# Two PSUM copies ahead of a cast, and a store, the turns and a load of rows moved into a y phase, in a two-layer spectral and MLP kernel

## The chip, the cores and the metric

The kernel runs on one core of one Trainium2 chip. The metric is the device time of the program in microseconds, the median of several runs. The core's engines work from queues of their own: TensorE (PE) multiplies, VectorE (DVE) and ScalarE (ACT) work element by element, GpSimd (POOL) takes small pieces, and SyncE (SP) issues every DMA of this kernel, in the order of the program.

## What is computed

```python
def _A_ref(x, dft_seq_re, dft_seq_im, dft_hid_re, dft_hid_im):
    a = jnp.einsum("bsd,ed->bse", x, dft_hid_re)
    b = jnp.einsum("bsd,ed->bse", x, dft_hid_im)
    y = jnp.einsum("ts,bse->bte", dft_seq_re, a) - jnp.einsum("ts,bse->bte", dft_seq_im, b)
    return y
def _B_ref(x, w1, w2, w3, w4):
    ...  # h = gelu(layernorm(x) @ w1), its four quarters shifted by +1, -1, +2, -2 rows
    x1 = x + hs                      # hs = shifted h @ w2
    return x1 + _gelu(_layernorm(x1, axis=-1) @ w3) @ w4
x = x + _A_ref(_layernorm(x, axis=-1), ...)
x = x + _B_ref(_layernorm(x, axis=-1), ...)
x = x + _A_ref(_layernorm(x, axis=-1), ...)
x = x + _B_ref(_layernorm(x, axis=-1), ...)
```

x is 1 x 2048 x 512 in 32-bit floats; the inner width of the MLP is 1376.

## The kernel before

**Precision.** Every operand is split into a high part (a cast to the fast 32-bit matmul type) and a low part (the rest). A product is three matmuls, high x high, high x low, low x high (`mm3`, L295 to L297), so PE's second matmul of a product is the first to read the streamed operand's low part.

**Fourier layers.** The kernel does the sequence transform first. It walks over 4 chunks of 512 output columns (c = 0 to 3), and in each chunk over 8 pairs of row tiles (k). Chunk 0 of layer 0 is a plain phase; every other chunk has an *x phase* (`x_phase`), then a *y phase* (`y_phase`). The two use sums and differences of the blocks of the sequence matrices, so that fewer products are needed. The phases share the eight PSUM banks, in pairs PA, PB, PC, PD (psa to psd in the profile). At the end of the x phase ACT copies PC, PB and PA to SBUF (L518, L520, L526), since the y phase writes the same banks anew. In the x phases of c = 1 to 3 also the hidden transform of the chunk before is computed (`hid`, on PD). The last chunk's hidden transform stands alone behind the last y phase: four pieces of the hidden matrices, 24 matmuls each (`HORDER`), with the left operands im0, re1, im1 and re0 (buffers rr) in this order. Then comes the MLP (`by_pairs`).

**The stream.** The blocks of the matrices come through a ring of 4 buffers. A piece is loaded into one of 4 raw buffers (6 from late in the x phase to the end of the y phase; raw_180 to raw_185 in the lists below) by `issue_dma`, L223, as soon as all users of the piece that had it have run. `stage_one` makes a block's high part. In the y phase it is a DVE subtraction of two raw halves (L247, written to ring...f) and an ACT cast (L248). `stage_two` makes the low part on DVE (L258). `stream()` hands PE the next block; before that it runs `stage_one` of the blocks ahead, up to 4 buffers, and `stage_two` of all but the newest. So on DVE the subtraction of a block stands ahead of the low part of the block before it. The y phase has 16 blocks, two a pair, of 12 matmuls each.

**Work beside the stream.** The program's order on each engine is written by hand: the phases call hooks between the blocks (`hook(i)` in the x phase with i = 2k and 2k + 1, `hook(k)` in the y phase). In layer 0 they also prepare sums of MLP weights that DRAM keeps for later: a *sum unit* is loaded, summed, split and stored (`sum_load`, `sum_make`, `sum_low`, `sum_keep`), at steps given to `sum_at`; step 16 + k lies in the y phase. The buffer suma of such a unit lies at the same SBUF address as turned0.

**In the last chunk** (c = 3) the hooks also start the MLP's input: rows of the finished sum x come back from DRAM (`BACK`: step of the x phase and first row tile), four row tiles are normalized (L354) and *turned* (32 x 32 block transposes on DVE, L632) into turned0, four DMAs store that to zd (`turn_out`, L642), and one load brings it back as the MLP's left operand (`turn_in`, L647, in the y phase's last hook).

Of the kernel before, what the change touches and what calls it, by code (L numbers as in the profile page):

```python
# [21 lines left out]
NC = S // CH  # L22
# [14 lines left out]
WARM = 12  # L37
X6, X7 = 2, 4
HAT = (2, 3, 3, 4, 5, 5, 6, 6)
BACK = {8: 0, 11: 2, 13: 4}  # L40
HORDER = ((1, 0), (0, 1), (1, 1), (0, 0))


# [1 line left out]
def spectral_mlp_kernel(ctx: ExitStack, tc: tile.TileContext, x, ws, hs, w1, w2, w34, out):  # L45
    nc = tc.nc
# [9 lines left out]
    x1d = dram.tile([S, D], F32, name="x1d")  # L56
# [28 lines left out]
    def at(name, word, *shape, dtype=F32R):  # L85
        return nc.alloc_sbuf_tensor_at(name, [P, *shape], dtype, offset=base + 4 * word).ap()
# [4 lines left out]
    tmp = at("tmp", TMP, 6, D, dtype=F32)  # L91
# [6 lines left out]
    xs = [at(f"xs{i}", XS + i * 2 * D, 2, D, dtype=F32) for i in range(NP)]  # L98
    turned0 = at("turned0", 5 * AY, KD, CH, dtype=F32)
# [25 lines left out]
    def xt(j):  # L125
        return xs[j // 2][:, j % 2]
# [22 lines left out]
    pieces, items, w_items, w_pieces, y_pieces = [], [], [], [], set()  # L149
# [43 lines left out]
            uses.setdefault(i, []).append((n, "two" if it[0] == "plain" else "one"))  # L193
    raws, slots, sums = {}, {}, {}
    held = {i: None for i in range(len(raw_at))}
    state = {"wide": False, "dma": 0, "one": 0, "two": 0, "use": 0, "made": 0, "done": 0, "limit": 0, "load": w_pieces[0]}
    x_left = [(0, 1), (1, 1)] + [(j, 2) for j in range(2, NT, 2)]

    def load_x():
        if x_left:  # L200
            j, n = x_left.pop(0)
            rows(xs[j // 2][:, j % 2 : j % 2 + n], x, j, n, True)

    def rows(sb, d, j, n, load):
        v = d[j * P : (j + n) * P, :].rearrange("(t p) d -> p t d", p=P)
        nc.sync.dma_start(*((sb, v) if load else (v, sb)))

    def issue_dma(upto=None):
        while state["dma"] < (state["load"] if upto is None else upto):
            i = state["dma"]  # L210
            free = [
                r
                for r, p in held.items()
                if (r < RAW or state["wide"] and i in y_pieces)
                and (p is None or all(n < state[stage] for n, stage in uses[p]))
            ]
            if not free:
                break
            src, a, b = pieces[i]
            r = min(free, key=lambda r: (-1 if held[r] is None else held[r], r))  # L220
            held[r] = i
            raws[i] = raw_at[r]
            nc.sync.dma_start(raws[i][:, a:b], src)  # L223
            state["dma"] += 1
            if i % 2 and i > 3:
                load_x()

    def stage_one():

        n = state["one"]  # L230
        kind, ids, (a, b), dest = items[n]
        issue_dma()
        if dest is None:
            dest = ring[state["made"] % RING]
            sums[n] = ringf[state["made"] % RING][:, :, 1]
            state["made"] += 1
        slots[n] = dest
        r = [raws[i] for i in ids]
        lo = sums.get(n)
        if kind == "plain":  # L240
            nc.scalar.copy(dest[:, a:b, 0], r[0][:, a:b])  # L241
        elif kind == "one":
            nc.vector.tensor_tensor(lo[:, 0], r[0][:, 1], r[0][:, 0], op=ALU.subtract)
            nc.scalar.copy(dest[:, 0, 0], lo[:, 0])  # L244
        else:
            i = 1 if kind == "by1" else 0
            nc.vector.tensor_tensor(lo, r[1][:, i : i + 1].broadcast_to([P, 2, CH]), r[0], op=ALU.subtract)  # L247
            nc.scalar.copy(dest[:, :, 0], lo)  # L248
        state["one"] += 1
        issue_dma()  # L250

# [18 lines left out]
    def prefetch():  # L270
        n = state["one"]
        while room():
            stage_one()
            while state["two"] < state["one"] - 1:
                stage_two()
        while state["two"] < n:
            stage_two()
# [5 lines left out]
    def stream():  # L283
        i = state["use"]
        if i and items[i - 1][3] is None:
            state["done"] += 1
        state["use"] += 1
        prefetch()
        while state["two"] <= i:
            stage_two()  # L290
        return slots.pop(i)
# [61 lines left out]
    def normed_act(o, s, mr):  # L353
        nc.scalar.activation(o, s, AF.Identity, bias=mr[2], scale=mr[1])  # L354
# [139 lines left out]
    def run_late(*names):  # L494
        for i in names:
            for f in late.pop(i, ()):
                f()

    def x_phase(c, hook):
        h = 0  # L500
        for k in range(NP):
            first, last = k == 0, k == NP - 1
            while c and h < NP and HAT[h] == k:
                s = stream()
                ri, dp = HORDER[h % 4]
                hid(ri, dp, s, PD, 2 * (h // 4), h % 4 == 0, h % 4 == 3)
                if h % 4 == 3:
                    at_mix = c == NC - 1 and h > 4
                    add_y(c - 1, h // 4, PD, X1 if h > 4 else X0, 2 * k + 1 if h < 4 else "y", "10" if at_mix else 2 * k + 2 if h < 4 else "y+")
                h += 1  # L510
            s = stream()
            run_late(2 * k)
            hook(2 * k)
            mm_half(PC, ax[k][:, 2], s[:, 0], first, last)
            mm_half(PB, ax[k][:, 1], s[:, 1], first, last)
            if last:
                for i in range(2):
                    nc.scalar.copy(im1s[:, i], PC[i])  # L518
                for i in range(2):
                    nc.scalar.copy(re1s[:, i], PB[i])  # L520
            s = stream()
            run_late(2 * k + 1)
            hook(2 * k + 1)
            mm_half(PA, ax[k][:, 0], s[:, 0], first, last)
        for i in range(2):
            nc.scalar.copy(re0s[:, i], PA[i])  # L526
# [64 lines left out]
    ln1, ln2 = {}, {}  # L591
# [35 lines left out]
    def blocks_of(u):  # L627
        return u.rearrange("p (d a i) -> p d a i", d=KD, a=NB)

    def turn_one(t, q, u):  # L630
        v = t.rearrange("p d (a q j) -> p d a q j", a=NB, q=TC)[:, :, :, q]
        nc.vector.transpose(v, blocks_of(u))  # L632

    def turn_out(t, to=None):

        if to is None:
            count["turn"] += 1
            to = zd[count["turn"] % 2]
        z = to.rearrange("(e i) t -> i e t", i=B)
        for b in range(NB):  # L640
            v = t[b * B : (b + 1) * B].rearrange("i d (a t) -> i (d a) t", a=NB)
            nc.sync.dma_start(z[:, :, b * P : (b + 1) * P], v)  # L642
# [973 lines left out]
    sum_a = [(*both("suma", 5 * AY, 4, 2, 2 * P), slice(0, 4))]  # L1616
# [45 lines left out]
    def sum_at(c, kind, k, places, *at_):  # L1662
        todo = (
            lambda: sum_load(kind, k, places),
            lambda: sum_make(kind, places),
            lambda: sum_low(places),
            lambda: sum_keep(kind, k, places),
        )
        for step, f in zip(at_, todo):
            prepare.setdefault((c, step), []).append(f)  # L1670
# [4 lines left out]

    for c, units in ((1, ((3, 0), (3, 1), (3, 2))), (2, ((3, 3), (3, 4), (4, 0))), (3, ((4, 1), (4, 2)))):
        sum_at(c, *units[0], sum_b, 5 if c == 1 else 0, 8 if c == 1 else 7, 9 if c == 1 else 8, 9)
        sum_at(c, *units[1], sum_a, 1, 10, 11, 12 if c == 3 else 21)
        if c < 3:
            sum_at(c, *units[2], sum_t, 11, 13, 14, 18)  # L1680
    sum_at("hid", 4, 3, sum_b, 0)
# [2 lines left out]
    for layer in range(LAYERS):  # L1684
# [4 lines left out]
        for c in range(NC):  # L1689
# [90 lines left out]
            def hook(i):  # L1780
# [34 lines left out]
                if i == 9:  # L1815
                    rows(X0, x1d, j, 2, False)
                if c == NC - 1 and i in BACK:
                    rows(xs[BACK[i] // 2], x1d, BACK[i], 2, True)
                if c == NC - 1 and i == 12:
# [5 lines left out]
            def hook(k):  # L1825
                if layer == 0:
                    prepare_at(c, 2 * NP + k)
                if layer and c == 0:
                    for step, f in zip((1, 1, 2), (ay_sums, ay_highs, ay_lows)):
                        if k == step:  # L1830
                            f(7)
                if k == 1 and c:
                    rows(X1, x1d, (c - 1) * TC + 2, 2, False)
                if c == NC - 1 and k < 2:
                    for q in (2 * k, 2 * k + 1):
                        turn_one(turned0, q, tmp[:, q])
                    for j in (2, 3)[: 2 - 2 * k]:
                        normed_act(tmp[:, j], xt(j), ln2[j])
                if c == NC - 1 and k == 2:
                    turn_out(turned0)  # L1840
                if c == NC - 1 and k == NP - 1:
                    turn_in(ztf[0])

# [7 lines left out]
        for i, (ri, dp) in enumerate(HORDER):  # L1851
# [8 lines left out]
            if i < 3:  # L1860
                j = (6, 8, 10)[i]
# [68 lines left out]
```

## Time and profile before

| | us |
|---|---|
| median of 3 runs | 1419.08 (1418.76 to 1419.23) |
| the profiled execution: its own time | 1418.97 |
| the profiled execution: span of its instructions | 1417.2 |

The span runs from the first to the last instruction in the trace; 1.8 us of the execution's time lie outside it. Times of the trace are microseconds from the span's start. A row of the timeline gives start, length, engine, line, operation, output <- inputs, shapes, the number of merged instructions (xN), and in brackets how long the engine was idle before it and what ended that. A length runs from an instruction's start to its end; a matmul of 512 columns shows 0.39, but the next starts 0.23 after it, since they are pipelined. The length in a row of SP is that of the issue alone; when the data have landed is told by the line "DMA to landing".

### The profile page before, as it was taken

To read this page: it belongs to the slowest core of one execution; us is meant where nothing else is said; L and a number is where in the kernel's file an instruction comes from. 1 tells how busy PE (TensorE), PEld (TensorE's weight loads), DVE (VectorE), ACT (ScalarE), POOL (GpSimd) and SP (SyncE) were. 2 spreads that over 40 slices of the span, in tenths; PEclk is the share of its full clock that TensorE was granted. 3 is DMA by queue.
4 is the path that set the end of the run, shared out by engine and by line. 5 is a ranking of instruction groups with operands and counts; after the bars stand their busy time and mean duration, and the time that the engine had idled before them with its cause. 6 is when DMAs were issued, how large, how long until landed. Compare 5 with 4: busy or idle time off the path is not lost.

```text
span 1417.2 us, 18479 instructions
## 1 busy us (share of the span) xinstructions
PE 1409.0 (99%) x6669; PEld 1181.8 (83%) x6669; DVE 1191.3 (84%) x1684; ACT 765.5 (54%) x1072; POOL 68.2 (5%) x105
## 2 busy tenths in 40 slices
PE   9999999999999999999999999999999999999998
PEld 8888788888788888988888888888888888899887
DVE  7988998998988789956789979879889788897776
ACT  6664555556566655534555545645555566454351
POOL 2100000000001100000000000000000020000000
PEclk9999999999999999999999999999999999999999
DMA  8978858778774748865556476565587457687864
GB/s 290 306 236 302 268 194 274 241 230 309 255 228 146 253 165 264 257 247 180 195 177 218 136 225 206 166 220 170 193 265 237 134 141 245 188 250 252 297 205 160
DMA packets 158907, 316.18 MB, mean 223 GB/s; under 512 B 10848, under 2 KB 78816, under 8 KB 156896
## 3 DMA queue, kind: packets, MB, share of 16 engines
q1 hardware_dynamic: 158816, 315.01, 67.9%
q8 instruction: 52, 0.85, 0.2%
q14 instruction: 39, 0.32, 0.1%
HBM read 260.70 MB, written 54.26 MB: 222 GB/s over the span
## 4 chain that ended last, share of the span: by engine, by line
PE 94%; DVE 3%; DMA 1%; ACT 1%; issue 1%; SPq 0%; POOL 0%; DVEq 0%; ACTq 0%; POOLq 0%
PE psd L295 10%; PE psd L296 10%; PE psd L297 10%; PE psa L295 8%; PE psa L297 8%; PE psa L296 8%; PE psb L296 7%; PE psb L297 7%; PE psb L295 7%; PE psc L295 6%; PE psc L296 6%; PE psc L297 6%; DMA raw<-in_ws 1%; DVE ring L258 1%; DVE rest L492 0%
## 5 line engine op out<-in xcount | busy, mean ns | idle before, releaser
L241 ACT CAST ring<-raw 128x1024 fp32r<-128x1024 f32 x127 | 132.9, 1052 | 69.4 <-PE psd L297 30.6
L258 DVE TENSOR_TENSOR ring<-raw,ring 128x1024 fp32r<-128x1024 f32 x126 | 153.4, 1220 | 14.3 <-ACT ring L241 14.3
L295 PE MATMUL psd<-ring,rr 128*128 128x512 f32 x208 | 80.9, 389 | 0.0
L296 PE MATMUL psd<-ring,rr 128*128 128x512 f32 x208 | 80.9, 389 | 0.0
L297 PE MATMUL psd<-ring,rr 128*128 128x512 f32 x208 | 80.9, 389 | 0.0
L248 ACT CAST ring<-ring0f 128x1024 fp32r<-128x1024 f32 x28 | 29.5, 1054 | 46.9 <-DVE ring0f L247 46.9
L258 DVE TENSOR_TENSOR ring<-ring1f,ring 128x512 fp32r<-128x512 f32 (+1 forms) x56 | 53.3, 952 | 0.8 <-ACT ring L244 0.7
L346 POOL TENSOR_TENSOR rows<-ve,mhalf 128x4 f32<-128x4 f32 x16 | 18.2, 1136 | 735.2 <-DVE ve L345 735.2
L295 PE MATMUL psc<-ring,ay 128*128 128x512 f32 x128 | 50.0, 391 | 1.6 <-ACT rr11f L518 1.6
L296 PE MATMUL psb<-ring,ay 128*128 128x512 f32 x128 | 50.0, 391 | 1.2 <-DVE ring L258 1.2
L297 PE MATMUL psb<-ring,ay 128*128 128x512 f32 x128 | 49.8, 389 | 0.0
L295 PE MATMUL psb<-ring,ay 128*128 128x512 f32 x128 | 49.8, 389 | 0.0
L296 PE MATMUL psc<-ring,ay 128*128 128x512 f32 x128 | 49.8, 389 | 0.0
L297 PE MATMUL psc<-ring,ay 128*128 128x512 f32 x128 | 49.8, 389 | 0.0
L297 PE MATMUL psa<-ring,ay 128*128 128x512 f32 x126 | 49.0, 389 | 0.0
L295 PE MATMUL psa<-ring,ay 128*128 128x512 f32 x126 | 49.0, 389 | 0.0
L295 PE MATMUL psd<-ring,ay 128*128 128x512 f32 x126 | 49.0, 389 | 0.0
L296 PE MATMUL psd<-ring,ay 128*128 128x512 f32 x126 | 49.0, 389 | 0.0
L296 PE MATMUL psa<-ring,ay 128*128 128x512 f32 x126 | 49.0, 389 | 0.0
L297 PE MATMUL psd<-ring,ay 128*128 128x512 f32 x126 | 49.0, 389 | 0.0
L314 POOL TENSOR_TENSOR rs<-ve,mhalf 128x2 f32<-128x2 f32 (+2 forms) x33 | 28.5, 863 | 412.4 <-DVE nb L313 393.4
L697 DVE TENSOR_TENSOR rg<-gt,rg 128x512 fp32r<-128x512 f32 x32 | 22.1, 690 | 29.6 <-ACT rg L696 29.6
(834 smaller groups left out, 4617.1 us busy)
## 6 DMA issues: line engine op xcount, KB each, us to landing
raw<-in_ws SPq DMA_DIRECT2D x183, 512.0 KB, 5.4
raw<-in_hs SPq DMA_DIRECT2D x56, 512.0 KB, 3.7
w3b<-w3d SPq DMA_DIRECT2D x11, 1792.0 KB, 8.5
w4r<-w4d SPq DMA_DIRECT2D x22, 512.0 KB, 3.5
un<-w4s SPq DMA_DIRECT2D x40, 256.0 KB, 3.7
un<-w4d SPq DMA_DIRECT2D x38, 256.0 KB, 4.4
x1d<-tmp SPq DMA_DIRECT2D x12, 512.0 KB, 6.8
xs<-x1d SPq DMA_DIRECT2D x12, 512.0 KB, 5.2
```

Of the source, the lines that this page charges most:

```text
L241: nc.scalar.copy(dest[:, a:b, 0], r[0][:, a:b])
L248: nc.scalar.copy(dest[:, :, 0], lo)
L258: nc.vector.tensor_tensor(lo, src, hi.bitcast(F32), op=ALU.subtract)
L295: nc.tensor.matmul(o, lh, rh, start=first, stop=False, skip_group_check=more)
L296: nc.tensor.matmul(o, lh, rl, start=False, stop=False, skip_group_check=more)
L297: nc.tensor.matmul(o, ll, rh, start=False, stop=last, skip_group_check=more)
L314: nc.gpsimd.tensor_tensor(rs[:, :n], ve[:, :n], mhalf[:, 0, :n], op=ALU.pow)
L346: nc.gpsimd.tensor_tensor(rs, ve, mhalf[:, :, :2], op=ALU.pow)
L697: nc.vector.tensor_tensor(lo, src, hi.bitcast(F32), op=ALU.subtract)
```

## The change

The two copies of PC at the end of each x phase go ahead of the cast of the y phase's second block: a block's cast is put in a list, and run at once unless `hold` is set, as it is in the last k of an x phase. The store of the last suma unit, (4, 2), goes from step 12 (x phase of chunk 3) to step 18 (y phase, k = 2). The load of row tiles 4 and 5 into xs[2] leaves the x phase (step 13) and goes into the y phase at k = 3, in both layers. In layer 0 the turns go from k = 0 and 1 to k = 3 and 5, and their store from k = 2 to k = 5; in layer 1 they stay. No work is added or removed.

```diff
-BACK = {8: 0, 11: 2, 13: 4}
+BACK = {8: 0, 11: 2}
...
+    casts = []
+
+    def cast_held():
+        while casts:
+            casts.pop(0)()
...
-            nc.scalar.copy(dest[:, :, 0], lo)
+            casts.append(lambda: nc.scalar.copy(dest[:, :, 0], lo))
+            if not state["hold"]:
+                cast_held()
...
+            state["hold"] = last
             s = stream()
...
             if last:
                 for i in range(2):
                     nc.scalar.copy(im1s[:, i], PC[i])
+                state["hold"] = False
+                cast_held()
                 for i in range(2):
                     nc.scalar.copy(re1s[:, i], PB[i])
...
-        sum_at(c, *units[1], sum_a, 1, 10, 11, 12 if c == 3 else 21)
+        sum_at(c, *units[1], sum_a, 1, 10, 11, 18 if c == 3 else 21)
...
-                if c == NC - 1 and k < 2:
-                    for q in (2 * k, 2 * k + 1):
-                        turn_one(turned0, q, tmp[:, q])
-                    for j in (2, 3)[: 2 - 2 * k]:
-                        normed_act(tmp[:, j], xt(j), ln2[j])
-                if c == NC - 1 and k == 2:
-                    turn_out(turned0)
+                if c == NC - 1:
+                    turns = (0, 1, 2) if layer else (3, 5, 5)
+                    if k in turns[:2]:
+                        for q in (0, 1) if k == turns[0] else (2, 3):
+                            turn_one(turned0, q, tmp[:, q])
+                    if not k:
+                        for j in (2, 3):
+                            normed_act(tmp[:, j], xt(j), ln2[j])
+                    if k == turns[2]:
+                        turn_out(turned0)
+                if c == NC - 1 and k == 3:
+                    rows(xs[2], x1d, 4, 2, True)
```

The lists below show what stands on an engine one behind the other. Line numbers of the changed program are its own (L254 there is L248 before, L266 is L258, L253 is L247, L643 is L632, L653 is L642).

ACT at the end of chunk 3's x phase in layer 0, before: psc is PC, psb is PB, ring...f the differences of the y phase's blocks.

```order
L248 CAST ring_172<-ring0f 128x2x512
L248 CAST ring_174<-ring1f 128x2x512
L518 COPY rr11f<-psc_249 128x512
L518 COPY rr11f<-psc_250 128x512
L520 COPY rr01f<-psb_247 128x512
```

The same place in the changed program:

```order
L254 CAST ring_172<-ring0f 128x2x512
L527 COPY rr11f<-psc_249 128x512
L527 COPY rr11f<-psc_250 128x512
L254 CAST ring_174<-ring1f 128x2x512
L531 COPY rr01f<-psb_247 128x512
```

The cast of block 1 went behind the two copies of psc; the same holds at all seven ends of x phases.

SP at the same place, before: w4s<-suma is the sum unit's store, xs_147<-x1d the load of rows, raw_184 and raw_185 take the pieces of the y blocks 4 and 5.

```order
L223 DMA raw_183<-in_ws 128x1024
L1655 DMA w4s_87<-suma 128x2048
L1598 DMA w3d_83<-tmp 256x1x256
L206 DMA xs_147<-x1d 128x2x512
L223 DMA raw_184<-in_ws 128x1024
L223 DMA raw_185<-in_ws 128x1024
```

And changed:

```order
L223 DMA raw_183<-in_ws 128x1024
L1609 DMA w3d_83<-tmp 256x1x256
L223 DMA raw_184<-in_ws 128x1024
L223 DMA raw_185<-in_ws 128x1024
L223 DMA raw_180<-in_ws 128x1024
```

The store and the load of rows went out from ahead of raw_184; the short store w3d<-tmp stayed.

SP further on in chunk 3's y phase, before: raw_180 and raw_181 here take the pieces of pair 6 (blocks 12 and 14), zd<-turned are the turns' four stores, in_hs is the hidden matrices.

```order
L206 DMA x1d<-tmp 128x2x512
L223 DMA raw_180<-in_ws 128x1024
L223 DMA raw_181<-in_ws 128x1024
L642 DMA zd_73<-turned_153 32x16x128 x4
L223 DMA raw_182<-in_ws 128x1024
L223 DMA raw_183<-in_ws 128x1024
L223 DMA raw_180<-in_hs 128x1024
L223 DMA raw_181<-in_hs 128x1024
```

And changed:

```order
L206 DMA x1d<-tmp 128x2x512
L223 DMA raw_180<-in_ws 128x1024
L223 DMA raw_181<-in_ws 128x1024
L1666 DMA w4s_87<-suma 128x2048
L223 DMA raw_182<-in_ws 128x1024
L223 DMA raw_183<-in_ws 128x1024
L206 DMA xs_147<-x1d 128x2x512
L653 DMA zd_73<-turned_153 32x16x128 x4
L223 DMA raw_180<-in_hs 128x1024
L223 DMA raw_181<-in_hs 128x1024
```

The sum unit's store now stands where the turns' stores stood, and these stand directly ahead of the hidden matrices.

DVE in the same y phase, before: the first turns stand ahead of the subtraction of block 4.

```order
L258 TENSOR_TENSOR ring_176<-ring2f,ring_176 128x2x512
L632 STREAM_TRANSPOSE turned_153<-tmp 128x16x32 x2
L247 TENSOR_TENSOR ring0f<-raw_185,raw_184 128x2x512
L258 TENSOR_TENSOR ring_178<-ring3f,ring_178 128x2x512
L247 TENSOR_TENSOR ring1f<-raw_185,raw_184 128x2x512
```

In the changed program they stand behind the low part of block 8 (ring_172), and ahead of the subtraction of block 10 (ring2f):

```order
L266 TENSOR_TENSOR ring_172<-ring0f,ring_172 128x2x512
L643 STREAM_TRANSPOSE turned_153<-tmp 128x16x32 x2
L253 TENSOR_TENSOR ring2f<-raw_185,raw_184 128x2x512
L266 TENSOR_TENSOR ring_174<-ring1f,ring_174 128x2x512
L253 TENSOR_TENSOR ring3f<-raw_185,raw_184 128x2x512
L266 TENSOR_TENSOR ring_176<-ring2f,ring_176 128x2x512
L500 TENSOR_TENSOR rr00f<-rr00f,rr11f 128x2x512
```

The first of these transposes waits for the store w4s<-suma, before and after. The second pair went from behind the low part of block 4 to behind that of block 12. PE's and POOL's lists are the same in both programs.

## Rows read from the trace of the kernel before

**Rows 1.** The page, part 1: busy time, share of the span, instructions

```profile
PE 1409.0 (99%) x6669; PEld 1181.8 (83%) x6669; DVE 1191.3 (84%) x1684; ACT 765.5 (54%) x1072; POOL 68.2 (5%) x105
```

**Rows 2.** PE's waits, whole span: total us, times, longest

```profile
PE psc L295 <- ACT rr11f L518: 1.6, 2, 0.8
...
PE psb L296 <- DVE ring L258: 1.2, 1, 1.2
```

**Rows 3.** Timeline of PE, chunk 1's and chunk 2's change to y

```profile
148.16 0.39 PE L297 MATMUL psa<-ring,ax 128*128 128x512 f32 x1
149.31 0.50 PE L295 MATMUL psc<-ring,ay 128*128 128x512 f32 x1 [0.76 <-ACT rr11f L518]
...
152.42 0.40 PE L296 MATMUL psb<-ring,ay 128*128 128x512 f32 x1
...
251.55 0.40 PE L296 MATMUL psb<-ring,ay 128*128 128x512 f32 x1
```

**Rows 4.** Timeline of ACT, chunk 1's change to y

```profile
148.68 1.07 ACT L518 COPY rr11f<-psc 128x512 f32<-128x512 f32 x2
```

**Rows 5.** Timeline of DVE, chunk 1's and chunk 2's change to y

```profile
150.96 1.22 DVE L258 TENSOR_TENSOR ring<-ring1f,ring 128x1024 fp32r<-128x1024 f32 x1
...
250.07 1.22 DVE L258 TENSOR_TENSOR ring<-ring1f,ring 128x1024 fp32r<-128x1024 f32 x1
```

**Rows 6.** Timelines of ACT and DVE, layer 1, chunk 1's change to y

```profile
849.52 1.05 ACT L248 CAST ring<-ring1f 128x1024 fp32r<-128x1024 f32 x1 [0.68 <-DVE ring1f L247]
...
851.69 1.22 DVE L258 TENSOR_TENSOR ring<-ring1f,ring 128x1024 fp32r<-128x1024 f32 x1
```

**Rows 7.** Timeline of PE, chunk 3's y phase and the hidden phase's first matmul

```profile
346.57 0.39 PE L295 MATMUL psc<-ring,ay 128*128 128x512 f32 x1
...
354.73 0.39 PE L295 MATMUL psb<-ring,ay 128*128 128x512 f32 x1
356.27 0.50 PE L296 MATMUL psb<-ring,ay 128*128 128x512 f32 x1 [1.15 <-DVE ring L258]
...
391.94 0.39 PE L295 MATMUL psc<-ring,rr 128*128 128x512 f32 x1
```

**Rows 8.** Timeline of DVE, chunk 3's y phase

```profile
349.86 1.22 DVE L258 TENSOR_TENSOR ring<-ring2f,ring 128x1024 fp32r<-128x1024 f32 x1
350.99 1.30 DVE L632 STREAM_TRANSPOSE turned<-tmp 128x512 f32<-128x512 f32 x2
353.86 1.23 DVE L247 TENSOR_TENSOR ring0f<-raw,raw 128x1024 f32<-128x1024 f32 x1 [1.57 <-DMA raw<-in_ws]
```

**Rows 9.** Timeline of SP, end of chunk 3's x phase

```profile
341.45 1.02 SPq L1655 DMA_DIRECT2D w4s<-suma  x1
343.52 0.52 SPq L1598 DMA_DIRECT2D w3d<-tmp  x1
...
345.62 0.95 SPq L223 DMA_DIRECT2D raw<-in_ws  x1
```

**Rows 10.** Chunk 2's loads; landings of L1655's stores issued 262.46, then 341.45

```profile
261.61 0.81 SPq L223 DMA_DIRECT2D raw<-in_ws  x2
...
DMA to landing us min/median/max: 9.2/9.2/9.2
...
DMA to landing us min/median/max: 7.3/7.3/7.3
```

**Rows 11.** SP, the turns' stores; landings of L223's loads issued 367.87, then 380.21

```profile
364.02 3.73 SPq L642 DMA_DIRECT2D zd<-turned  x4
...
DMA to landing us min/median/max: 7.4/7.4/7.4
...
DMA to landing us min/median/max: 3.6/3.6/3.6
```

**Rows 12.** Timelines of ACT and DVE, start of the hidden phase: parts of im0

```profile
387.37 1.05 ACT L450 CAST rr<-rr10f 128x1024 fp32r<-128x1024 f32 x1
...
388.46 1.23 DVE L453 TENSOR_TENSOR rr<-rr10f,rr 128x1024 fp32r<-128x1024 f32 x1
```

More of the change, by code (lines that the diff above doesn't have):

```diff
@@ L195, in spectral_mlp_kernel @@
     held = {i: None for i in range(len(raw_at))}
-    state = {"wide": False, "dma": 0, "one": 0, "two": 0, "use": 0, "made": 0, "done": 0, "limit": 0, "load": w_pieces[0]}
+    state = {"wide": False, "hold": False, "dma": 0, "one": 0, "two": 0, "use": 0, "made": 0, "done": 0, "limit": 0, "load": w_pieces[0]}
     x_left = [(0, 1), (1, 1)] + [(j, 2) for j in range(2, NT, 2)]
```

## The prediction

> **What bounds the kernel now.** I read the busy times first: TensorE (PE) is busy for 1409.0 of 1417.2 us, and DVE for 84% [rows 1]. So a change of order can win only the time in which PE stands still, about 8 us, part of it at the start and in the MLP. The list of PE's waits says where the rest lies: two waits of the psc banks for ACT's copies (L518) and one of a psb bank for DVE's L258 [rows 2]. They fall at the end of the x phases of chunks 1 and 2 of layer 0, and in the y phase of chunk 3. The timeline of PE gives their size. At chunk 1 the next matmul comes 1.15 us after the one before it, where 0.23 is usual, so 0.92 is lost, and 0.11 more because a matmul after a wait takes 0.50 instead of 0.39 [rows 3]. Chunk 2 is built alike. In chunk 3 the y phase starts at 346.57 and its blocks take 2.72 each (354.73 less 346.57, over three blocks). Without a wait the hidden phase would begin after 16 blocks, at 390.09; it begins at 391.94 [rows 7]. So 1.85 us are lost there, and all three places together hold about 3.95 us: the most that the change can give.
>
> I number the 16 y blocks of a chunk from 0. Block n needs sub(n) (DVE, L247), cast(n) (ACT, L248) and low(n) (DVE, L258). In program order sub(n+1) stands ahead of low(n), and PE's second matmul of block n, 0.23 after its first, needs low(n). A DVE operation starts 1.14 after the one before (349.86 to 350.99) and ends 1.22 after its start [rows 8].
>
> **The copies ahead of the cast.** At chunk 1 ACT copies psc at 148.68, behind a cast [rows 4]. With the copies first PE may start block 0 about 0.9 us earlier. But then DVE ends the gain: its order and its work are untouched, it runs without a gap here, and low(1) runs from 150.96 to 152.18 [rows 5]. PE's second matmul of block 1 is now at 152.42 [rows 3]; it can come down to 152.23 (0.05 from DVE to PE, as from DVE's low(3), which ended at 356.22 by the spacing above, to PE at 356.27), and then pays the 0.11 of a restart. That is a gain of 0.08. At chunk 2 low(1) ends at 251.29 against 251.55 on PE [rows 3, 5]: a gain of 0.10. Together 0.2 of the 2.1 us that lie there; I take 0.2, because DVE's rows are closer than the wait's own length, and keep 2.1 as the other end. The same swap at chunk 3 and four times in layer 1 costs nothing: in layer 1 the cast starts at 849.52, could move by the 1.07 of two copies at most, and would end at 851.64; DVE reads it at 851.69 [rows 4, 6]. PE has no wait there now [rows 2].
>
> **The store and the load out of the x phase.** In chunk 3 SP issues the sum unit's store (1.02), a short store that waits for DVE until 343.52, the load of rows, and only then, at 345.62, the loads for blocks 4 and 5 [rows 9]. Their landing ends DVE's idle 1.57 us ahead of sub(4) at 353.86, behind the first two turns (1.30) [rows 8]. Without them the loads go out from 344.1, the second at 344.5. Now they are there at 353.86, 8.24 after the first's issue; even with that they would land at 352.3, and low(3) would end 1.14 + 1.22 later, at 354.7. PE wants it at 354.96, 0.23 into block 3. Without the store and the rows ahead of them they should be earlier, about when DVE comes free of low(2), at 351.0. So the whole 1.85 us goes. (The short store keeps its place: the loads can't go earlier than 344.1.)
>
> **The store in the y phase.** It lies now behind the two loads for pair 6 (blocks 12 and 14), and these wait for sub(7). From sub(4) at 351.0, six operations of 1.14 later sub(7) starts at 357.85 and ends at 359.1. The first two turns write the memory that the store reads, so DVE waits at them until it has landed; behind them on DVE stand sub(10) and low(9). How long that is, the same place in chunk 2 shows: two loads at 261.61, a store of the same 1 MB behind them, landed 9.2 after its issue at 262.46, so 10.05 after the first load [rows 10]. That gives 369.15 here. The other bound is the store as it is now, 7.3 after its issue [rows 10]: 359.95 + 7.3 = 367.3. I take the first, which has the same two loads ahead. When must the turns start? Block 9 starts at 346.57 + 9 x 2.72 = 371.05, its second matmul at 371.28; turns 1.21, sub(10) 1.14, low(9) 1.22 and 0.05 to PE make 3.62. So 367.66. The wait costs 369.2 - 367.66 = 1.55, with the restart 1.66 (0 at the lower bound). DVE then has 2.72 - 2.28 = 0.44 a block to catch up; in blocks 10 to 13 it has also an add (L492, 1.14) and the second pair of turns (1.21) to do, 2.35 against 1.76. That is 0.6 more, as one or two short waits.
>
> The Trainium skill ("DMA: Bandwidth & Descriptors", Anatomy of one DMA — SWDGE (gpsimd) path) prices a DMA at about 2.0 us plus its bytes at 436 GB/s; this is for the other issuing path. An estimate by it is 4.4 us for this 1 MB, a landing at 364.4 and no wait. The trace does not agree: it shows 7.3 and 9.2.
>
> **The turns' own store.** The second pair of turns comes nine DVE operations behind the first: 369.2 + 1.21 + 9 x 1.14 = 380.65, ended at 381.95. Then SP issues the four stores of turned rows (3.73) and only then the first load of the hidden weights, which now lies far behind them [rows 11]. It goes out at 385.7 and lands, at the 3.6 it takes on an idle queue, at 389.3 [rows 11]. ACT's next cast waits for it, and behind that cast stand two copies and the cast of im0 (L450): 1.05 + 1.0 + 1.05, so im0's high part is there at 392.5, its low part (L453, 1.23) at 393.8 [rows 12]. PE reaches the hidden phase at 390.09 + 1.66 + 0.6 = 392.35 and reads the low part 0.45 later, at 392.8: about 0.15 for the one, 0.7 for the other, 0.2 for two restarts, and some 0.4 for the copies and re1 behind. Taken: 1.5. Now im0 has room: high part begun at 387.37, low part at 388.46, for 391.94 [rows 7, 12]. Bounds: 0, if the turns start early; and if the load lands as it did behind these stores in the y phase, 7.4 after its issue [rows 11], 3.8 more. I take the lower landing, since nothing else is queued by then. The load of rows itself, 0.5 MB between loads that have time, costs nothing in either layer; layer 1 keeps its turns.
>
> **Sum.** Gone: 1.85 + 0.2. New: 1.66 + 0.6 + 1.5 = 3.76. Net +1.7 on the profiled execution's 1418.97, or 1420.7; the median of the runs is 0.11 above that execution. Forecast 1420.8.
>
> **Rivals.**
> - The store lands in time (turns not held, start by 366). DVE's own pace would have them at 365.2. Then 2.05 us are won and about 0.1 comes back in the hidden phase: 1417.1. For it: the 7.3 us row is near; against it: the chunk 2 row, with the same neighbours. The price that the Trainium skill states above would give this case. 0.13.
> - The turns wait, but the hidden phase has enough room: +2.26 - 2.05 = +0.2, 1419.3. For it: the first of its waits comes out at only 0.15; against it: the low part follows 1.3 behind the high part. 0.14.
> - Slower: the first load of hidden weights is held by the turns' stores and lands late. At half way between 3.6 and 7.4 us it adds 1.9: 1422.7. It decides from a landing at about 390.5 on. For it: the one row of a load behind such stores; against it: that load had two others ahead. 0.20.
> - The copies pay in full (2.1) and the store lands in time: 1415.2. Against it: DVE's unbroken row of work. 0.03.
> - The forecast, 1420.8, own range 1419.8 to 1421.9: 0.50. That the change doesn't do what it says is excluded by the order: only these instructions move, PE's order stays.
>
> **How the numbers follow.** About 0.2% (2.84 us) is what a measurement of this kernel can tell from no change, so the bounds are 1416.2 and 1421.9. Faster 0.03, slower 0.20, the three cases between 0.77. The range leaves out the 0.03 below and about half of the slower case: 1417.0 to 1422.6.
>
> **What would show it.** Right: at the ends of the x phases of chunks 1 and 2 PE waits for DVE L258 instead of ACT; no wait at 356; DVE idle some 4 us ahead of the first turns of layer 0, released by the store; a PE wait at about 371 and one at the start of the hidden phase on ACT or DVE. Wrong: the store landing before 367.6, or the hidden loads issued by 383; and if DVE's low(1) starts earlier than now, the copies are worth more than 0.2.

## The result, and the profile after

| | us | ratio to before, 95% interval |
|---|---|---|
| before, median of the runs beside it | 1418.76 | |
| after, median of 7 runs | 1423.27 (1422.79 to 1425.07) | 1.0032 (1.0022 to 1.0042) |
| after, the profiled execution (span) | 1425.07 (1423.1) | |

The change costs 4.5 us; the forecast was +1.7, its range ended at 1422.6. The profiled execution is the slowest of the seven; why, is told below.

PE's busy time and PE's waits in the profile of the changed kernel (total us, times, longest), beside [rows 1, 2]:

```profile
PE 1412.6 (99%) x6669; PEld 1182.2 (83%) x6669; DVE 1191.6 (84%) x1684; ACT 764.9 (54%) x1072; POOL 68.6 (5%) x105
...
PE psc L303 <- ACT rr L458: 2.6, 1, 2.6
PE psb L304 <- DVE ring L266: 2.5, 3, 1.7
```

The two waits for ACT's copies are gone. In their place stand short waits for DVE, one longer one, and a new one for the cast of im0 (L458). PE is also *busy* 3.6 us longer, with the same 6669 matmuls: some of them ran slower.

Timeline of PE (start, length, then as in the rows of before): the second matmul of block 1 at chunk 2, the first wait in chunk 3's y phase, and the start of the hidden phase.

```profile
250.77 0.50 PE L304 MATMUL psb<-ring,ay 128*128 128x512 f32 x1 [0.38 <-DVE ring L266]
...
372.50 0.50 PE L304 MATMUL psb<-ring,ay 128*128 128x512 f32 x1 [1.74 <-DVE ring L266]
...
394.69 0.80 PE L303 MATMUL psc<-ring,rr 128*128 128x512 f32 x1 [2.55 <-ACT rr L458]
395.28 0.63 PE L304 MATMUL psc<-ring,rr 128*128 128x512 f32 x1
395.95 0.80 PE L305 MATMUL psc<-ring,rr 128*128 128x512 f32 x1
396.54 0.63 PE L303 MATMUL psc<-ring,rr 128*128 128x512 f32 x1
396.97 0.63 PE L304 MATMUL psc<-ring,rr 128*128 128x512 f32 x1
397.40 0.63 PE L305 MATMUL psc<-ring,rr 128*128 128x512 f32 x1
```

No row like the second of these stands at 356 any more, where [rows 7] have the old wait. The hidden phase's matmuls are 0.63 or 0.80 long where the first one in [rows 7] has 0.39. The first three start 0.59 to 0.67 after one another, those from the fourth on 0.43, where 0.23 is usual. The table of stretches says why (busy us of each engine with its instructions, granted clock, DMA share, GB/s):

```profile
388.00:392.00 4.00, 4.00 (x19) 3.09 (x17) 1.82 (x2) 0.32 (x1) 0.00 (x0) 1.00 0.96 334
392.00:394.60 2.60, 0.14 (x1) 0.00 (x0) 1.23 (x1) 2.60 (x5) 0.00 (x0) 0.96 1.02 395
394.60:401.30 6.70, 6.57 (x15) 4.75 (x16) 6.53 (x6) 5.65 (x9) 0.00 (x0) 0.51 0.75 265
401.30:405.00 3.70, 3.70 (x18) 3.06 (x17) 2.58 (x3) 2.23 (x3) 0.00 (x0) 1.00 0.86 238
```

The granted clock falls late in the wait (0.96 over its 2.6 us), is 0.51, the 1.2 GHz level, over the next 6.7 us, and 1.00 again afterwards. The Trainium skill ("TensorE: Matmul & The Clock Gate", Wait — 56ns, not 53.3ns?) gives 426.7 ns from start to start for 512 columns at this level; the trace agrees with its 0.43.

DVE and SP: the first turns, and the turns' stores with the loads of the hidden matrices behind them. Below them, when the sum unit's store (issued at 359.09) and the first hidden load (384.86) have landed, counted from the issue.

```profile
368.90 1.30 DVE L643 STREAM_TRANSPOSE turned<-tmp 128x512 f32<-128x512 f32 x2 [4.13 <-DMA w4s<-suma]
...
381.64 3.12 SPq L653 DMA_DIRECT2D zd<-turned  x4
384.86 3.40 SPq L223 DMA_DIRECT2D raw<-in_hs  x4
...
DMA to landing us min/median/max: 9.8/9.8/9.8
...
DMA to landing us min/median/max: 6.4/6.4/6.4
```

To see where time comes and goes I set the same matmul of the two traces side by side, by its place in PE's order, and take the difference of the start times at the end of each section. This is the ledger, in us against the kernel before. "Start" is what the two executions differ by at 20 us (in the second trace of the changed kernel, by 100 us), ahead of all that was changed; it comes and goes from run to run.

| kernel | start | chunks 1, 2 | old wait, chunk 3 | store's wait | knock-ons | hidden phase |
|---|---|---|---|---|---|---|
| after | -0.52 | -0.16 | -1.84 | +2.03 | +0.53 | +6.09 |
| after, once more | +0.39 | -0.27 | -1.85 | +1.62 | +0.53 | +4.86 |

All the rest of the program changes it by less than 0.2. The first trace is that of the slowest run: by the medians (+4.5, of which the other columns make 0.56) the hidden phase costs about 4 in a usual run.

### The profile page after: what moved, and what is told of

The parts are those of the page before. It is cut to its first block, busy times and chain, and to the rows that moved or that the text cites. A ratio compares the mean times of both kernels' runs of the same rounds, so it can differ in the third digit from the quotient of the medians.

```text
span 1423.1 us, 18484 instructions
## 1 busy us (share of the span) xinstructions
PE 1412.6 (99%) x6669; PEld 1182.2 (83%) x6669; DVE 1191.6 (84%) x1684; ACT 764.9 (54%) x1072; POOL 68.6 (5%) x105
## 4 chain that ended last, share of the span: by engine, by line
PE 90%; DVE 5%; DMA 2%; issue 1%; ACT 1%; SPq 0%; DVEq 0%; POOL 0%; ACTq 0%; POOLq 0%
PE psd L303 9%; PE psd L305 9%; PE psd L304 9%; PE psa L305 8%; PE psa L303 8%; PE psa L304 8%; PE psb L304 6%; PE psb L305 6%; PE psb L303 6%; PE psc L303 6%; PE psc L305 6%; PE psc L304 6%; DVE ring L266 1%; DVE rest L500 1%; DMA w4s<-suma 1%
## 5 line engine op out<-in xcount | busy, mean ns | idle before, releaser
L247 ACT CAST ring<-raw 128x1024 fp32r<-128x1024 f32 x127 | 132.7, 1051 | 74.6 <-PE psd L305 29.1
L266 DVE TENSOR_TENSOR ring<-raw,ring 128x1024 fp32r<-128x1024 f32 x126 | 153.4, 1221 | 16.9 <-ACT ring L247 16.9
L266 DVE TENSOR_TENSOR ring<-ring1f,ring 128x512 fp32r<-128x512 f32 (+1 forms) x56 | 53.4, 953 | 0.8 <-ACT ring L250 0.7
L254 ACT CAST ring<-ring0f 128x1024 fp32r<-128x1024 f32 x28 | 29.5, 1054 | 45.5 <-DVE ring0f L253 45.5
```

The source lines that it names most:

```text
L254: casts.append(lambda: nc.scalar.copy(dest[:, :, 0], lo))
L266: nc.vector.tensor_tensor(lo, src, hi.bitcast(F32), op=ALU.subtract)
```

## The experiments

**The copies alone.** The changed kernel with the rest put back:

```diff
-BACK = {8: 0, 11: 2}
+BACK = {8: 0, 11: 2, 13: 4}
...
-        sum_at(c, *units[1], sum_a, 1, 10, 11, 18 if c == 3 else 21)
+        sum_at(c, *units[1], sum_a, 1, 10, 11, 12 if c == 3 else 21)
...
-                    turns = (0, 1, 2) if layer else (3, 5, 5)
+                    turns = (0, 1, 2)
...
-                if c == NC - 1 and k == 3:
-                    rows(xs[2], x1d, 4, 2, True)
```

> Only the two psc copies ahead of the y block's cast; the store, the turns and the load of rows stand where they stood in the kernel before. Theory (DVE's unbroken row of work ends the gain): in the trace of the changed kernel PE regains 0.04 us at chunk 1 and 0.08 at chunk 2, so here 0.12 us below the kernel before, about 1418.7, not to be told from no change; PE waits at chunk 1 and chunk 2 for DVE's low part (L266), and the wait of 1.8 us in chunk 3 is back. Rival (ACT's copies were what PE waited for, so the whole wait goes): 2.1 us below, about 1416.7.

Measured: 1418.7 against 1419.27, ratio 0.9995 (0.9986 to 1.0004). In the ledger -0.29 at chunks 1 and 2, and +0.16 in chunk 3, where the old wait for the loads is only reached sooner. So the copies give 0.13 by the trace, as expected; the medians can't tell it from no change.

**The same with one DVE operation taken out of the row.** To test that it is DVE which keeps the rest:

```diff
-            sum_at(c, *units[2], sum_t, 11, 13, 14, 18)
+            sum_at(c, *units[2], sum_t, 11, 13, 17, 18)
```

> The kernel with the copies alone, and the third sum unit's low part three steps later at chunks 1 and 2; chunk 3 as in the kernel before. Theory (the two copies give 0.12 alone because DVE's row of work holds PE next): with one DVE operation out of that row the waits at DVE's low part go, 0.64 at each of two chunks: 1.4 below the kernel before, about 1417.9. Rival (the copies' value was never there, PE's next limit is something else): 0.1 below, about 1419.2.

Measured: 1417.65 against 1418.87, 0.9990 (0.9981 to 0.9998). Its list of PE's waits keeps the one in chunk 3 alone:

```profile
PE psb L304 <- DVE ring L266: 1.4, 1, 1.4
PE psd L140 <- POOL ident masks.py:199: 1.4, 1, 1.4
```

The ledger has -1.57 at chunks 1 and 2. The theory holds: the value was there, 1.28 us of it, behind a DVE operation that PE does not need at that point.

**The store back in the x phase, the turns late.**

```diff
-        sum_at(c, *units[1], sum_a, 1, 10, 11, 18 if c == 3 else 21)
+        sum_at(c, *units[1], sum_a, 1, 10, 11, 12 if c == 3 else 21)
```

> The changed kernel with the last sum unit's store back in the x phase of chunk 3; the late turns and the late load of rows stay. Theory (the store's landing holds the turns, and all that follows comes of that): no DVE wait at the first turns, they start by 366, the turned rows are stored by 382, the hidden phase begins on time at full clock; the loads for blocks 4 and 5 go out 1.0 later than in the changed kernel, so of the old 1.85 us wait some 0.8 is back. Sum: 0.12 + 1.05 below the kernel before, about 1417.7. Rival (late turns by themselves make the hidden load late): the store's wait of 2.0 and the knock-ons of 0.5 go, a wait of 1.5 or more at the hidden phase stays, with the half clock behind it: 1420 to 1422.

Measured: 1421.04 against 1419.27, 1.0008 (0.9999 to 1.0016). The eleven runs spread from 1419.16 to 1421.87, and the traced one (1421.74) is among the slowest. My theory, 1417.7, fell: every run lies above it. The rival came out. DVE is not held at the turns, yet the hidden phase loses 4.18 in the ledger. At DVE's own pace the second turns end at 379.24; the stores go out until 382.4, and the first hidden load, issued at 382.49, lands 6.1 later:

```profile
DMA to landing us min/median/max: 6.1/6.1/6.1
```

The first and the third matmul of the hidden phase, and the stretches around its start (columns as above):

```profile
392.12 0.50 PE L303 MATMUL psc<-ring,rr 128*128 128x512 f32 x1 [1.45 <-ACT rr L458]
...
393.38 0.51 PE L305 MATMUL psc<-ring,rr 128*128 128x512 f32 x1 [0.53 <-DVE rr L461]
...
390.30:393.70 3.40, 1.42 (x5) 0.59 (x4) 2.71 (x3) 3.40 (x5) 0.00 (x0) 1.00 1.05 404
393.70:397.10 3.40, 3.40 (x9) 2.61 (x8) 3.30 (x4) 2.35 (x6) 0.00 (x0) 0.51 0.90 325
```

PE stood idle for 1.45 and once more for 0.53, and then had the half clock for 3.4 us. So late turns are enough to spoil the hidden phase; the store's wait only adds to their lateness. The 4.18 is this trace's: by the medians (+1.77, with 1.05 won ahead of it) the loss is about 2.8. Of the old wait 0.81 stays won, which I put down to the moved rows, and the other 1.03 to the store (its issue took 1.02 [rows 9]).

**The idle time filled.** To part the wait from the slow matmuls behind it:

```diff
+        if layer == 0:
+            for _ in range(11):
+                nc.tensor.matmul(PC[0], ay[7][:, 0, 0, :P], ay[7][:, 0].rearrange("p r d -> p (r d)"), start=True, stop=True)
         for i, (ri, dp) in enumerate(HORDER):
```

> The changed kernel with eleven more matmuls of 128x512 on PE, on operands that are there, into a bank that the hidden phase overwrites, between the last y block of layer 0 and the hidden phase: they fill the 2.7 us in which PE stands idle. Theory (the slow matmuls of the hidden phase come from the clock that fell when PE stood still): granted clock 1.0 throughout, the hidden phase's matmuls 0.227 us apart, its first real matmul again at about 394.7; the total is 2.8 us below the changed kernel's profiled run, that is some 3.2 above the kernel before by the trace. Rival (the matmuls are slow because the hidden loads and the turns' transfers crowd the memory that PE reads): 0.427 apart as before, the total stays at the changed kernel's 1423 to 1425.

Measured: 1422.97 against 1419.27, 1.0024 (1.0015 to 1.0033). Stretches with and behind the filling, and the first real matmuls:

```profile
391.20:394.00 2.80, 2.80 (x14) 2.24 (x13) 1.48 (x2) 2.80 (x5) 0.00 (x0) 1.00 1.00 383
394.00:401.00 7.00, 6.47 (x28) 4.44 (x26) 6.90 (x7) 5.56 (x8) 0.00 (x0) 1.00 0.79 272
```

```profile
393.86 0.41 PE L303 MATMUL psc<-ring,rr 128*128 128x512 f32 x1
394.11 0.40 PE L304 MATMUL psc<-ring,rr 128*128 128x512 f32 x1
395.03 0.50 PE L305 MATMUL psc<-ring,rr 128*128 128x512 f32 x1 [0.53 <-DVE rr L461]
395.36 0.39 PE L303 MATMUL psc<-ring,rr 128*128 128x512 f32 x1
395.60 0.40 PE L304 MATMUL psc<-ring,rr 128*128 128x512 f32 x1
```

The DMA share is 0.79 where the changed kernel had 0.75, the operands are the same, and the matmuls that don't wait run 0.23 to 0.25 apart at a clock of 1.00. So the slowness is the clock, not crowded memory, and it came of PE's standing still. The hidden phase costs 3.85 in this trace: that is the waits by themselves. The trace of the changed kernel lost 6.09 there. Of the 2.24 between them 0.22 lies ahead of the first real matmul (2.71 late there, 2.49 here, where the load landed sooner); the other 2.0 are the clock's.

The medians of the two kernels, however, lay only 0.3 apart (0.8, each counted from the kernel before that was measured beside it). So both ran once more side by side.

> The changed kernel once more, beside the run with the eleven filling matmuls on the same chip, to see how much of its loss the half clock is in a usual run. Its first profiled run lost 2.9 us at the half clock (granted clock of the run 0.997), its other runs showed 0.999 to 1.0. Theory (the clock falls for a stretch that differs from run to run): the median lies 0.8 to 1.5 us above the filled kernel's, and runs with a lower granted clock are the longer ones. Rival (the half clock is there for 6.8 us in every run): 2.8 us above the filled kernel's.

> The changed kernel with eleven filling matmuls in PE's idle time ahead of the hidden phase, again, on the same chip as the changed kernel. Theory: granted clock 0.999 or more in every run, 3.2 to 3.7 above the kernel before, 0.8 to 1.5 below the changed kernel. Rival: 2.8 below the changed kernel.

Measured: 1423.66 and 1423.04, against 1418.73 before (1.0032, 1.0020 to 1.0045, and 1.0027, 1.0017 to 1.0037). The clock costs 0.6 in a usual run, by these medians, less than the 0.8 to 1.5 that was expected, and the filled kernel lies 4.3 above the kernel before, not 3.2 to 3.7. The intervals overlap, so the traces carry this more than the times do. The runs of the changed kernel had a mean granted clock of 0.997 (1424.72 us), 0.998 (1423.80), 0.999 (1424.06, 1423.51, 1422.81) and 1.0 (1422.64): the lower the clock, the longer the run, by and large. In the new trace the half clock lasts about 3.4 us (0.53 over 3.60) instead of 6.8:

```profile
395.90:399.50 3.60, 3.58 (x9) 2.81 (x10) 3.50 (x4) 2.55 (x5) 0.00 (x0) 0.53 0.98 348
399.50:403.00 3.50, 3.50 (x17) 2.88 (x16) 3.45 (x3) 2.02 (x3) 0.00 (x0) 0.99 0.48 177
```

What decides its length was not tried.

**The turns' stores issued by POOL.** To take the hidden load out from behind them, in layer 0 alone (the part of the edit in `turn_out`):

```diff
-            nc.sync.dma_start(z[:, :, b * P : (b + 1) * P], v)
+            if pool:
+                for h in range(0, B, B // 2):
+                    nc.gpsimd.dma_start(z[h : h + B // 2, :, b * P : (b + 1) * P], v[h : h + B // 2])
+                continue
+            nc.sync.dma_start(z[:, :, b * P : (b + 1) * P], v)
```

> The changed kernel with the four stores of turned rows of layer 0 issued by POOL instead of SP (in eight halves), so that the loads of hidden weights do not stand behind them on SP. Theory (it is their place behind these stores that makes the hidden load late): the first hidden load goes out by 382 and lands by 386, no wait of PE at the hidden phase over 0.3 us, granted clock 1.0; the store's wait of 2.0 and the knock-ons of 0.5 stay. Sum 0.6 above the kernel before, about 1419.4. Rival (the stores' bytes crowd the load, whoever issues them): the load goes out early but lands after 389, and a wait of 1 us or more stays: 1421 or more. Second rival (im0 itself is late because DVE is late): the wait stays with the load landed early.

Measured: 1434.67 against 1419.27, 1.0106 (1.0091 to 1.0122). The load's landing, and ACT's cast of it:

```profile
DMA to landing us min/median/max: 4.0/4.0/4.0
```

```profile
386.10 1.05 ACT L247 CAST ring<-raw 128x1024 fp32r<-128x1024 f32 x1 [1.07 <-DMA raw<-in_hs]
...
416.64 2.12 ACT L458 CAST zt<-zt0f 128x1024 fp32r<-128x1024 f32 x2 [17.38 <-DMA zt0f<-zd]
418.67 1.04 ACT L458 CAST rr<-rr00f 128x1024 fp32r<-128x1024 f32 x1
```

The first part is as the theory says: the load goes out at 381.64, lands at 385.6, and at the start of the hidden phase PE does not wait. The total missed by 15 us, for a reason that neither side named. POOL's stores go out one behind the other:

```profile
393.96 0.57 POOL L655 DMA_DIRECT2D zd<-turned  x1 [2.71 <-issue]
397.31 0.57 POOL L655 DMA_DIRECT2D zd<-turned  x1 [2.78 <-issue]
400.85 0.57 POOL L655 DMA_DIRECT2D zd<-turned  x1 [2.97 <-issue]
```

The last lands at 410.5, the turned rows are back at 416.6, and ACT's cast of them stands ahead of the cast of re0, the last operand of the hidden phase. PE waits 11.9 us for it, and has the half clock behind that (0.50 from 412.5 to 426.2). So the turned rows have a second deadline, through ACT's order. This run says where the load must not stand, and is no way to mend it.

**Only the second turns one pair earlier.** The same question without POOL, and with the store's wait left in:

```diff
-                    turns = (0, 1, 2) if layer else (3, 5, 5)
+                    turns = (0, 1, 2) if layer else (3, 4, 4)
```

> The changed kernel with the store where the change puts it, and only the second turns and their stores one pair earlier. Theory (the hidden phase's loss hangs on the hidden load behind the stores of turned rows, not on DVE's lateness behind the store): the wait at the first turns stays, 2.0 us of PE; the add and the second turns now follow closer, 0.5 to 0.9 in knock-ons; the stores of turned rows go out at about 376, the hidden load by 382, and PE waits less than 0.5 at the hidden phase, at full clock. Sum 0.9 above the kernel before, about 1420.1. Rival (DVE's lateness itself makes im0 late): a wait of 1.5 or more at the hidden phase with the load landed by 387: 1422 or more.

Measured: 1419.6 against 1418.87, 1.0001 (0.9992 to 1.0010). PE's waits in chunk 3's y phase, and the landing of the first hidden load:

```profile
372.34 0.50 PE L304 MATMUL psb<-ring,ay 128*128 128x512 f32 x1 [1.64 <-DVE ring L266]
379.20 0.50 PE L304 MATMUL psb<-ring,ay 128*128 128x512 f32 x1 [1.11 <-DVE ring L266]
```

```profile
DMA to landing us min/median/max: 3.5/3.5/3.5
```

The store still holds DVE (4.02 us of idle time), and the knock-on grows to 1.4, where 0.5 to 0.9 was expected. But the load is now issued at 382.58, behind stores that have all landed, takes 3.5, and the hidden phase costs 0.0 in the ledger. DVE's lateness alone doesn't make im0 late: the load does.

**The store earlier too, and the best of both.**

```diff
-        sum_at(c, *units[1], sum_a, 1, 10, 11, 18 if c == 3 else 21)
+        sum_at(c, *units[1], sum_a, 1, 10, 11, 16 if c == 3 else 21)
...
-                    turns = (0, 1, 2) if layer else (3, 5, 5)
+                    turns = (0, 1, 2) if layer else (3, 4, 4)
```

> The changed kernel with the last sum unit's store two steps earlier (at the y phase's first pair, ahead of the loads for block 10) and the second turns and their stores one pair earlier; still all of it in layer 0's last y phase. Theory (only the times at which the store lands and the turned rows go out spoil the change): the store goes out at about 349.3 and lands by 359.5, DVE is not held at the first turns (364.8), the second turns end by 374, the first hidden load goes out by 382 and lands by 386.5, no wait of PE at the hidden phase and no half clock. All of the old 1.85 us wait and 0.12 of the copies stay won: 1.97 below the kernel before, about 1417.2. Rival (the store now stands ahead of the loads for block 10, which then land late): a wait of 1 us or more in the y phase, the same time as the kernel before or above.

> As the run with the early store and turns, and the low part of the third sum unit of chunks 1 and 2, one DVE operation of 1.14 us, three steps later (behind the second pair of the y phase), so that DVE reaches the y phase's first blocks 1.14 earlier. Theory (DVE's unbroken row, not ACT's copies, is what now holds PE there): the waits of PE at DVE's low part fall from 0.64 with the restart to none at both chunks, another 1.2 us: 3.2 below the kernel before, about 1416.0. Rival (the operation is missed in the y phase, where DVE has 0.44 us a block to spare): waits there in its place, no further gain, 1417.2.

The second has the sum unit's low part at step 17 besides. Measured: 1416.58 and 1415.5 against 1418.87, that is 0.9981 (0.9972 to 0.9989) and 0.9971 (0.9960 to 0.9983): 2.3 and 3.4 below the kernel before, where 2.0 and 3.2 were expected. In the first, the store's landing, the first turns without idle time, the landing of the first hidden load, and the first matmul of the hidden phase:

```profile
DMA to landing us min/median/max: 9.1/9.1/9.1
...
364.68 1.30 DVE L643 STREAM_TRANSPOSE turned<-tmp 128x512 f32<-128x512 f32 x2
...
DMA to landing us min/median/max: 3.6/3.6/3.6
...
389.40 0.39 PE L303 MATMUL psc<-ring,rr 128*128 128x512 f32 x1
```

The store takes nearly as long as in the changed kernel, but from 349.36. In the second kernel, PE waits nowhere from its warm-up to the end; the list has one entry:

```profile
PE psd L140 <- POOL ident masks.py:199: 1.4, 1, 1.4
```

All the ledgers:

| kernel | start | chunks 1, 2 | old wait, chunk 3 | store's wait and knock-ons | hidden phase |
|---|---|---|---|---|---|
| copies alone | -0.21 | -0.29 | +0.16 | 0 | 0 |
| copies, low part later | -0.01 | -1.57 | +0.26 | 0 | 0 |
| store in the x phase | -0.38 | -0.24 | -0.81 | 0 | +4.18 |
| filled | -0.43 | -0.28 | -1.85 | +1.99 | +3.85 |
| filled, once more | -0.43 | -0.27 | -1.85 | +2.01 | +3.80 |
| stores by POOL | -0.40 | -0.27 | -1.85 | +1.45 | +16.03 |
| second turns earlier | -0.46 | -0.28 | -1.84 | +3.36 | 0 |
| store and turns earlier | -0.45 | -0.24 | -1.84 | 0 | 0 |
| the same, low part later | +0.20 | -1.64 | -1.85 | 0 | 0 |

The two kernels of the last lines beat both the kernel before and the changed one.

## Why the prediction was wrong

- **The copies.** Forecast 0.2, measured 0.16 to 0.29. DVE's row of work ended the gain, as written.
- **The wait in chunk 3.** Forecast 1.85, measured 1.84. The loads for blocks 4 and 5 came early enough: DVE's idle time ahead of that block is 0.34 instead of 1.57 [rows 8].
- **The store's wait.** The landing was put at 369.15, from the row of chunk 2 [rows 10]; it came at 368.88, DVE stood idle 4.13 where "some 4 us" was written, and the wait with its knock-ons is 2.56 (2.15 in the second trace) against 2.26. That the landing fits so closely is in part luck: the two loads ahead went out 0.9 earlier than forecast (358.23, not 359.1), and the store took 9.8 instead of 9.2. In the six traces with the store at this place it took 8.7 to 9.8.
- **The hidden phase.** This is the term that failed: 1.5 against 6.09 (4.86 in the second trace, about 4 by the medians). It rested on one choice, the load's landing: 3.6 after its issue, "since nothing else is queued by then". But the four stores were queued, directly ahead. The last of them, issued at 383.51, landed 4.7 later, at 388.2, and the load 3.0 after that, 6.36 after its own issue. [Rows 11] held the other end, 7.4, and I set it aside because two more loads stood ahead in that row; without these it still took 6.0 to 6.4 in five traces. The rest of the chain was right. Here it is on ACT:

```profile
391.68 1.04 ACT L247 CAST ring<-raw 128x1024 fp32r<-128x1024 f32 x1 [5.54 <-PE psa L305]
392.63 1.07 ACT L560 COPY tmp<-psd 128x512 f32<-128x512 f32 x2
393.58 1.05 ACT L458 CAST rr<-rr10f 128x1024 fp32r<-128x1024 f32 x1
```

From landing to im0's high part I had 3.2 us (389.3 to 392.5); it took 3.4 (391.22 to 394.63). The load landed 1.9 later than forecast, and PE came 0.4 earlier, so 0.15 became 2.7. The first row's bracket names PE, but the cast starts 0.46 after the load's landing, as it does in the kernel with POOL's stores, where the bracket names the DMA. The bracket is inferred; where two events lie close together, the landing has to be looked up.
- **The clock.** No term stood for it. The wait of 2.6 us let the granted clock fall, which made the hidden phase dearer by 2.0 in the first trace and by 1.2 in the second (behind the first matmul, against the filled kernel), and by about 0.6 in the medians. Even without it the sum would have been, by the filled kernel's ledger, -2.1 + 2.0 + 3.85 = +3.7, about 1422.5.
- **The rivals.** The "slower" rival had the mechanism. That it also has the landing nearly to the hundredth (half way between 3.6 and 7.4 after 385.7 is 391.2; measured 391.22) is luck: the load went out 0.84 earlier, at 384.86, and took 0.86 longer, 6.36 instead of 5.5. It had a chance of 0.20 where the case for it was the only row of such a load. Its price, 1.5 + 1.9 = 3.4, comes near the 3.85 of the waits alone; the clock took it further, to 1423.27. The rival "the store lands in time" allowed 0.1 for the hidden phase; the run with the store in the x phase shows 4.18 there in its trace, some 2.8 by the medians. I had asked when the first turns run and not when the second ones end.
- **The signs.** All that were to show it right came out: PE's waits for DVE at chunks 1 and 2, none at 356, DVE's 4.13, a wait at 372.5, and one for ACT at the hidden phase. They say where PE waits and not how long, so they couldn't tell the forecast from the slower rival.
- **The idea itself** is sound, which was not in the prediction: with the store two steps and the second turns one pair earlier, the 2.1 that it removes (0.24 + 1.84) stays removed.

## What to carry to other kernels

When a transfer is moved, follow every transfer that then stands behind it on the same queue to its reader, and take the landing of such a follower from the row that has the same neighbours ahead, even if other things differ; "nothing else is queued" has to be read off the order. A wait on PE of a few microseconds is to be priced at more than its length, since the matmuls behind it may run at the half clock (here they did after 2.55 and 2.15, and not after 1.74). And a group of steps that is put off together has as many deadlines as it has readers: here the first turns', the second turns' (through the stores and the hidden load) and the turned rows' own.

## What the runs showed of the hardware

- **A load behind stores of short rows.** Half a megabyte took 6.0 to 6.4 us from its issue in the five traces where four stores of 256 KB in rows of 512 bytes were still under way ahead of it, and 3.5 to 3.8 where they had landed. It landed 2.6 to 3.0 after the last of them each time. The Trainium skill ("DMA: Bandwidth & Descriptors", Queues, rings and completion order) says that each DMA engine takes the descriptors of a ring in order; the traces agree. The load's issue alone took 1.37 in the changed kernel, and 0.35 with the second turns earlier.
- **Stores issued by POOL.** Each of the eight 128 KB stores was issued 0.3 us after the one before had landed, one every 3.3 us or more; the same bytes issued by SP landed within 6.6 us in all.
- **The half clock's length.** It lasted about 6.8 us after an idle time of PE of 2.55; 3.4 after 2.15 and, two matmuls later, 0.52; 3.4 after 1.45 and, two matmuls later, 0.53; and 13.7 around one of 11.9. The clock stayed at 1.00 through a wait of 1.74 in the changed kernel, and of 1.64 and 1.11, 6.9 apart, with the second turns earlier.
